# A two-part kernel with a new threshold, shorter routing steps, deferred packing and more output buffers

## The chip, the cores and the metric

The kernel runs on one core of one Trainium2 chip. The metric is the device time of one execution in microseconds; before the change it is 294.05 us (median of three runs, 293.16 to 296.08). TensorE is granted one of two clocks, 1.2 or 2.4 GHz; the profile writes them as 0.50 and 1.00.

## What is computed

A decayed linear attention (4 batches, 8 heads, 768 positions, head size 64) gives 3072 rows of 512 values. A gate gives each row eight logits. All 3072 x 8 logits are walked in falling order, and a row goes to an expert as long as the row is free and the expert has fewer than 384 rows. Each expert is a two-layer network.

```python
    logits = x @ w_gate
    order = np.argsort(-logits.flatten())
    for idx in order:
        tok, e = (int(idx) // E, int(idx) % E)
        if assigned[tok] >= 0 or counts[e] >= cap:   # cap = N // E = 384
            continue
        assigned[tok] = e
        counts[e] += 1
    for e in range(E):
        mask = assigned == e
        h = np.maximum(x[mask] @ w1[e], 0.0)
        out[mask] = h @ w2[e]
```

## The kernel before

**Attention (`_Attn`).** 24 blocks g of 128 rows, six to a batch. Each block is a chain of some thirty operations on all engines: loads on SyncE's queue, splits into high and low halves on ScalarE, VectorE and GpSimd (`sp` lines 1235, 1241 and 1246, `ql` 1218, `xl` 1297, `stl` 1332, `kf` 1161, `vs` 1175, `vl` 1186), matmuls on TensorE, the result `xs` (1277), its store to `x_dram` (1282), and the gate logits, copied by ScalarE (line 1309). The order on each engine is made ahead by `_Plan`: each operation has an engine, a duration, what it depends on and a priority `OFF[name] + g * PERIOD`, and a list scheduler takes the ready operation that can start first. `Router.plan` puts the routing's steps into the same plan, with priorities from `at(g, t)`.

**Early routing (`_Router`).** Column t holds the rows of block t, one on each partition. `scale` (line 113) finds the range of the logits of 8 columns. `level` (line 155) counts how many best logits of 12 columns lie above each of 128 levels (comparison on line 170, twelve matmuls on line 174) and picks the threshold `tau` that 85% pass; lines 187 to 193 make the scale of the digits. A row whose best logit passes goes to its best expert at once; the others are "the rest" and are routed later. `sure` makes the one-hot G of expert or rest, and running counts; `slots` turns them into a place by matmuls (238 to 244) and makes A (line 260), BJ (264), the row numbers R1 (269) and the rows R of the rest (272 to 278); `digits` writes each logit as two half-precision numbers (289 to 302 on VectorE, 289 to 306 on GpSimd for the last two columns). This is done for columns 0 to 15, then 16 to 21. `pack` multiplies A with R1 (line 316) and with R (319) on TensorE; `rows` gives the row numbers of the first 256 rows of each expert, with which GpSimd gathers the rows of jobs 0 and 1 (line 709). Columns 22 and 23 come through `late`, one by one.

**Experts (`_Moe`, `_route_and_moe`).** Jobs 0 to 7 are 256 rows of each expert, jobs 8 to 15 the other 128. A job transposes its rows (727), copies them (`xeT`, 731), multiplies with w1 (745) into PSUM tiles S0 and S1, copies with ReLU (`hT`, 750), multiplies with w2 (761), copies to `oe` (766, ScalarE) and scatters to the output (767, GpSimd). Each `oe` tile is one of four buffers. Gathers, scatters and the loads of the weights (696, 16 of 1 MB) are all issued by GpSimd in order. Meanwhile `steps` routes the rest in seven rounds on VectorE, whose small matmuls are put between the experts' at planned distances (`WAIT`); it gives `perm2`, with which job 8 can gather. `finish` gets the packed sums, and the flag that it leads to sends the kernel into the slow `_exact_path` when a count was out of its bounds.

## Time and profile before

| | us |
|---|---|
| median of three runs | 294.05 |
| lowest, highest | 293.16, 296.08 |
| the profiled execution, device time | 292.14 |
| the profiled execution, span of its instructions | 290.3 |
| mean granted clock in it | 0.92 |

Busy time in the profiled execution: TensorE 231.2 us (80% of the span), VectorE 175.1 (60%), ScalarE 155.2 (53%), GpSimd 180.6 (62%). 52.03 MB are moved. A busy share is a mean over stages with different limits; the rows below are therefore cut into stages. A row of a timeline gives start, duration, engine, line, operation, output<-inputs, shapes and count, and in brackets how long the engine stood idle before and what ended that. One of a wait list gives who waited for whom, the sum, the times and the longest.

### The profile page before, as it was taken

The numbers are of one execution on the slowest core, as the hardware profiler recorded it, in microseconds if no ns is written. First come the engines' busy times: TensorE is split into PE (matmuls) and PEld (weight loads), VectorE is DVE, ScalarE is ACT, GpSimd is POOL, SyncE is SP. The second block draws the span as 40 slices with busy tenths as digits, with TensorE's granted clock in tenths as the row PEclk, the third lists the DMA queues.
The fourth block names the chain that finished last, engine by engine and source line by source line (L and its number), as shares of the span: only waits on it lengthen the run. The fifth ranks groups of instructions, "written<-read, shape, count | busy, mean of one in ns | idle before, by whom it ended". The sixth has DMA issues, their size and how long they took to land.

```text
span 290.3 us, 8655 instructions
## 1 busy us (share of the span) xinstructions
PE 231.2 (80%) x3458; PEld 182.5 (63%) x3471; DVE 175.1 (60%) x572; ACT 155.2 (53%) x297; POOL 180.6 (62%) x225
## 2 busy tenths in 40 slices
PE   1689897999997995985874887886577899899980
PEld 0568786888886875875873645654345566577740
DVE  2569786688989869899955477785566470000000
ACT  5388786788887754673210335325242354466650
POOL 9789798889979965876437783425352145454220
PEclk9999998899999996999555699999998899999996
DMA  6999999999999938999983999999999426333111
GB/s 132 217 218 212 212 234 241 250 232 242 223 262 243 252 91 178 150 216 185 223 177 43 152 190 208 225 228 229 225 232 227 150 86 133 92 92 78 71 76 42
DMA packets 96975, 52.03 MB, mean 179 GB/s; under 512 B 76960, under 2 KB 88224, under 8 KB 96928
## 3 DMA queue, kind: packets, MB, share of 16 engines
q0 software_dynamic: 17920, 26.22, 47.2%
q1 hardware_dynamic: 79008, 25.19, 39.2%
q8 instruction: 29, 0.48, 0.7%
q14 instruction: 18, 0.15, 0.2%
HBM read 58.74 MB, written 12.58 MB: 246 GB/s over the span
## 4 chain that ended last, share of the span: by engine, by line
PE 38%; DMA 20%; DVE 14%; issue 11%; POOL 8%; ACT 5%; SPq 1%; POOLq 0%; ACTq 0%; DVEq 0%
DMA out_dram<-oe,perm 12%; DMA w<-in_moe_w_dram 6%; PE p L761 5%; PE p L745 5%; PE S L1228 5%; PE XL L1268 4%; PE n L1191 3%; PE pt L1191 3%; PE stp L1319 3%; PE pos L1191 3%; POOL xe L709 3%; DVE sp L1241 3%; PE XL L1257 2%; DVE xs L1277 2%; DMA kf<-in_k_dram 2%
## 5 line engine op out<-in xcount | busy, mean ns | idle before, releaser
L745 PE MATMUL p<-xeT,w 128*128 128x256 bf16 (+1 forms) x512 | 51.7, 254 | 8.6 <-ACT hT L750 5.7
L745 PEld LDWEIGHTS <-w 128*128 128x128 bf16 x512 | 40.2, 100 | 17.5 <-issue 10.8
L761 PE MATMUL p<-w,hT 128*128 128x512 bf16 x179 | 45.4, 379 | 7.0 <-ACT oe L766 6.3
L767 POOL DMA_INDIRECT out_dram<-oe,perm x24 | 24.2, 1007 | 41.8 <-ACT oe L766 33.9
L750 ACT ACTIVATE hT<-p 128x512 bf16<-128x512 f32 (+1 forms) x64 | 31.0, 491 | 20.4 <-PE p L745 18.7
L1235 ACT CAST sp<-S 128x512 bf16<-128x512 f32 x48 | 33.7, 747 | 15.2 <-PE S L1228 8.6
L1246 POOL TENSOR_SCALAR_AFFINE_SELECT sp<-sp 128x512 f32<-128x512 f32 x48 | 30.7, 646 | 12.3 <-DVE sp L1241 9.4
L766 ACT COPY oe<-p 128x512 f32<-128x512 f32 x24 | 14.0, 585 | 45.2 <-PE p L761 22.1
L709 POOL DMA_INDIRECT xe<-x_dram,perm x24 | 24.7, 1029 | 21.3 <-PE p L745 4.8
L1241 DVE TENSOR_TENSOR sp<-S,sp 128x512 bf16<-128x512 f32 x48 | 33.7, 741 | 4.2 <-ACT sp L1235 3.5
L761 PEld LDWEIGHTS <-hT 128*128 128x128 bf16 x192 | 16.7, 97 | 23.0 <-issue 8.3
L1161 POOL TENSOR_TENSOR kf<-kf 128x512 f16<-128x512 f32 x24 | 25.9, 1079 | 8.2 <-DMA kf<-in_k_dram 8.2
L1186 POOL TENSOR_TENSOR vl<-vs,vh 128x512 bf16<-128x512 f32 x24 | 27.9, 1161 | 4.0 <-ACT vh L1181 3.7
L1175 POOL TENSOR_TENSOR vs<-vf,lamneg 128x512 f32<-128x512 f32 x24 | 25.1, 1045 | 0.0
L1228 PE MATMUL S<-qh,kT 64*128 64x128 f16 x384 | 22.7, 232 | 1.9 <-DVE sp L1241 1.3
L1268 PE MATMUL XL<-vh,sp 128*128 128x64 bf16 x384 | 23.9, 198 | 0.3 <-POOL sp L1246 0.3
L1277 DVE TENSOR_TENSOR xs<-XL,lampow 128x512 f32<-128x512 f32 x24 | 16.5, 687 | 11.0 <-PE XL L1268 10.9
L1191 PE MATMUL pt<-identf,qf 128*128 128x128 f32 x96 | 16.7, 301 | 8.0 <-DMA qf<-in_q_dram 8.0
L1268 PEld LDWEIGHTS <-sp 128*128 128x128 bf16 x576 | 21.5, 101 | 2.3 <-POOL sp L1246 0.8
L1228 PEld LDWEIGHTS <-kT 64*128 64x128 bf16 (+1 forms) x576 | 18.4, 102 | 5.5 <-issue 3.8
L1268 PE MATMUL XL<-vl,sp 128*128 128x64 bf16 x192 | 21.6, 198 | 0.0
L1191 PE MATMUL n<-identf,xs 128*128 128x128 f32 x96 | 16.7, 300 | 4.2 <-DVE xs L1277 2.1
(269 smaller groups left out, 536.7 us busy)
## 6 DMA issues: line engine op xcount, KB each, us to landing
w<-in_moe_w_dram POOLq DMA_DIRECT2D x16, 1024.0 KB, 14.2
qf<-in_q_dram SPq DMA_DIRECT2D x24, 256.0 KB, 5.1
kf<-in_k_dram SPq DMA_DIRECT2D x24, 256.0 KB, 5.0
vf<-in_v_dram SPq DMA_DIRECT2D x24, 256.0 KB, 5.0
x_dram<-xs SPq DMA_DIRECT2D x24, 256.0 KB, 4.6
xe<-x_dram,perm POOLq DMA_INDIRECT x24, 5.8
out_dram<-oe,perm POOLq DMA_INDIRECT x24, 3.2
lam_sb<-in_lam_dram SPq DMA_DIRECT2D x1, 4.0 KB, 3.1
```

Source lines behind the costliest of these rows:

```text
L709: nc.gpsimd.indirect_dma_start(out=xe[:, c, :], out_offset=None, in_=self.x_dram[0:rows, :], in_offset=bass.IndirectOffsetOnAxis(ap=pm, ax ...
L745: nc.tensor.matmul(p1[:, f, 0:n, :], self.w1t[e][:, kc, fc * P : (fc + 1) * P], j["xeT"][:, kc, 0:n, :], start=(kc == 0), stop=(kc == 3), ...
L750: nc.scalar.activation(hT[:, fp, :, 0:n, :], p1[:, :, 0:n, :], ACT.Relu)
L761: nc.tensor.matmul(p2, j["hT"][:, kc // 2, kc % 2, c, :], self.w2t[e][:, kc, :], start=(kc == 0), stop=(kc == 7), skip_group_check=True)
L1161: self.nc.gpsimd.tensor_tensor(lo, kf.rearrange("p (c j) -> p c j", c=4), self.ksplit(kf)[0], OP.subtract)
L1186: self.nc.gpsimd.tensor_tensor(d["vl"], d["vs"], d["vh"], OP.subtract)
L1191: self.nc.tensor.transpose(ps[:, hp, :], src(hp), self.identf)
L1228: self.nc.tensor.matmul(S[a][:, hp, :], kk[r, hp, :], qq[r, hp, :], start=(i == 0), stop=(i == 2))
L1235: self.nc.scalar.copy(s[:, :, :, 1], d["S"][a])
L1241: self.nc.vector.tensor_tensor(s[:, :, :, 0], d["S"][a], s[:, :, :, 1], OP.subtract)
L1246: self.nc.gpsimd.affine_select(out=sf, in_=sf, compare_op=OP.is_ge, fill=0.0, base=0, pattern=[[0, 4], [1, 128]], channel_multiplier=-1)
L1268: self.nc.tensor.matmul(d["XL"][:, a, hp, :], d["sp"][a][:, hp, :, ss], vv[:, 2 * hp + a, :], start=(first and hp == 0 and i == 0), stop=( ...
```

## The change

- `level` takes the mean over the partitions of the least best logit in columns 0 to 4 as threshold, by one matmul with a matrix of 1/128. `scale` loses its own search and takes its range from the same matmul; it runs as one step after it.
- `sure` compares the logits with max(best, threshold) and has no more index arithmetic. `digits` has four steps in place of seven and runs on VectorE alone, for columns 0 to 21 after the attention (`at(24, 0)`); the rows of the rest (`rest_rows`) are moved there too. Slots are made for columns 0 to 17 and 18 to 21 (before 0 to 15 and 16 to 21).
- `pack` does only the product with R1; the product with R (`gain`) goes into `finish`, and both accumulators share the bank `cnt`.
- `late` is gone: columns 22 and 23 are one piece with the same functions, in `finish`.
- `warm(n)` puts n matmuls of 512 columns, whose result nobody reads, on TensorE: 4, 8 and 6 of them in `finish`, ahead of the transposes of job 0.
- `oe` has seven buffers instead of four.
- PERIOD is 4.4 instead of 4.6, and all offsets are new. Some constants are gone.

```diff
-    NR, NB, CA, CB = 8, 12, 16, 22
+    NR, CA, CB = 5, 18, 22
+    MID, SPAN, TOP = 1536.0, 2.25, 2047.0
...
+    def level(self, L):
...
+        V.reduce_max(self.v[:, 0:n], L[:, 0:n, :], axis=AX.X)
+        yield
+        m2 = rc.tile([P, 2], F32, name="m2")
+        V.tensor_reduce(m2[:, 0:1], self.v[:, 0:n], axis=AX.X, op=OP.min)
+        V.tensor_reduce(m2[:, 1:2], L[:, 0:n, :].rearrange("p t e -> p (t e)"), axis=AX.X,
                         op=OP.min)
         yield
...
+        tp = self.ps.tile([P, 2], F32, tag="cnt", name="tps")
+        nc.tensor.matmul(tp, self.mean, m2, start=True, stop=True)
+        yield
+        self.tb = rc.tile([P, 2], F32, name="tb")
+        V.tensor_copy(self.tb, tp)
+        self.tau = self.tb[:, 0:1]
+
+    def scale(self):
...
+        V.tensor_scalar(zr, self.tb[:, 1:2], self.tau, -self.SPAN, OP.subtract, OP.mult)
+        V.tensor_scalar(zr, zr, 1e-30, None, OP.max)
         self.zlo = rc.tile([P, 1], F32, name="zlo")
...
+        V.tensor_tensor(self.zlo, zr, self.tau, OP.subtract)
         self.zsc = rc.tile([P, 1], F32, name="zsc")
         V.reciprocal(self.zsc, zr)
...
+        V.tensor_scalar(self.zsc, self.zsc, self.TOP, None, OP.mult)
...
+        V.tensor_scalar(u, v, self.tau, None, OP.max)
         yield
         G = rc.tile([P, 9, n], BF16, name=f"G{k}")
...
+        V.tensor_tensor(G[:, 0:8, :], L[:, a:b, :].rearrange("p t e -> p e t"),
+                        u[:, None, :].to_broadcast([P, 8, n]), OP.is_ge)
+        yield
+        V.tensor_scalar(G[:, 8, :], v, self.tau, None, OP.is_lt)
         yield
...
+    def digits(self, L, a, b):
...
+        V.tensor_scalar(Z, L[:, a:b, :].rearrange("p t e -> p e t"), self.zlo, self.zsc, OP.add,
+                        OP.mult)
+        yield
+        V.tensor_scalar(Z, Z, 1.0 / 1024.0, self.TOP, OP.max, OP.min)
+        yield
+        zh = self.zp[:, :, 0, a:b]
+        V.tensor_copy(zh, Z)
+        yield
+        V.tensor_tensor(self.zp[:, :, 1, a:b], Z, zh, OP.subtract)
+        yield
...
     def pack(self, a, b):
 
         nc = self.nc
         if a == 0:
-            self.pe1 = self.ps.tile([128, 16], F32, tag="S0", name="pe1")
-            self.acc = self.ps.tile([128, 76], F32, tag="cnt", name="acc")
+            ct = self.ps.tile([128, 96], F32, tag="cnt", name="pk")
+            self.pe1, self.acc = ct[:, 0:16], ct[:, 16:92]
         for t in range(a, b):
             nc.tensor.matmul(self.pe1, self.A[:, :, t], self.R1[:, :, t], start=(t == 0),
                              stop=(t == self.CB - 1))
+
+    def gain(self, a, b):
+
         for t in range(a, b):
-            nc.tensor.matmul(self.acc, self.A[:, :, t], self.R[:, :, t], start=(t == 0), stop=False,
-                             skip_group_check=True)
+            self.nc.tensor.matmul(self.acc, self.A[:, :, t], self.R[:, :, t], start=(t == 0),
+                                  stop=(t == 23), skip_group_check=True)
...
+        plan.op("sc", 0, "DVE", 0.8, self.scale, [("rs", 3)], self.at(A, 5))
+        chain("d1", self.digits(L, 0, B), (0.35, 0.35, 0.3, 0.35), [("lg", B - 1), ("sc", 0)],
+              self.at(24, 0))
+        chain("x1", self.rest_rows(0, B), (0.5, 1.0), [("s2", 6), ("d1", 3)], self.at(24, 1))
...
+    def warm(self, n):
+        if n:
+            sink = self.ps.tile([128, 512], F32, tag="S1", name="sink")
+        for _ in range(n):
+            self.nc.tensor.matmul(sink, self.identb, self.i_kt.rearrange("p k t -> p (k t)")[:, 0:512],
+                                  start=True, stop=True)
+
     def finish(self, L):
...
+        self.gain(0, B)
+        list(self.sure(L, B, 24, 3))
+        self.warm(4)
+        yield 0.1
+        list(self.slots(B, 24, 3))
+        list(self.digits(L, B, 24))
+        list(self.rest_rows(B, 24))
+        self.warm(8)
+        yield 0.1
+        self.gain(B, 24)
...
+        self.warm(6)
         yield from self.steps(rest)
...
-        oe = self.mp.tile([P, 512], F32, tag="oe", name="oe", bufs=4)
+        oe = self.mp.tile([P, 512], F32, tag="oe", name="oe", bufs=7)
...
-            yield ("land", 0.5)
+            yield ("land", 1.0)
...
-    PERIOD = 4.6
...
+    PERIOD = 4.4
```

## Rows read from the trace of the kernel before

**Rows 1.** The page, chain of work that ended last: shares of the span by engine.

```profile
PE 38%; DMA 20%; DVE 14%; issue 11%; POOL 8%; ACT 5%; SPq 1%; POOLq 0%; ACTq 0%; DVEq 0%
```

**Rows 2.** Stretches: length, busy time (instructions) of each engine, clock, DMA share, GB/s.

```profile
63.83:87.16 23.33, 22.28 (x508) 19.90 (x509) 21.23 (x44) 20.00 (x41) 21.32 (x26) 1.00 1.02 243
87.16:102.70 15.54, 14.04 (x325) 12.45 (x325) 14.64 (x23) 11.93 (x25) 15.35 (x18) 1.00 1.05 248
102.70:112.78 10.08, 6.53 (x111) 4.77 (x109) 7.88 (x13) 3.60 (x8) 6.44 (x8) 0.89 0.55 106
112.78:151.88 39.10, 32.06 (x592) 28.78 (x590) 34.24 (x83) 18.68 (x38) 22.95 (x32) 0.76 1.02 192
151.88:161.38 9.50, 4.07 (x29) 3.20 (x29) 4.23 (x33) 1.18 (x2) 7.00 (x13) 0.50 0.42 53
161.38:231.67 70.29, 55.40 (x463) 37.02 (x469) 45.26 (x264) 25.86 (x41) 31.62 (x33) 0.95 1.10 211
231.67:249.92 18.25, 15.82 (x122) 10.63 (x122) 5.65 (x41) 9.20 (x15) 8.33 (x10) 1.00 0.41 101
249.92:290.30 40.38, 30.85 (x343) 22.32 (x347) 0.00 (x0) 19.71 (x47) 12.80 (x13) 0.93 0.26 74
```

**Rows 3.** Timelines of VectorE and of GpSimd in block 16.

```profile
105.23 0.29 DVE L178 TENSOR_SCALAR_CACHE_REDUCE lscr<-lcnt 128x128 bf16<-128x128 f32 x1 [2.09 <-PE lcnt L174]
107.66 3.97 DVE L189 SCALAR_TENSOR_TENSOR zlo<-zr,mb 128x1 f32<-128x1 f32 x1
...
110.97 0.63 POOL L1246 TENSOR_SCALAR_AFFINE_SELECT sp<-sp 128x512 f32<-128x512 f32 x1
```

**Rows 4.** Timelines of ScalarE, TensorE and GpSimd before the hand-over.

```profile
140.73 0.18 ACT L1309 COPY logits<-n 128x8 f32<-128x8 f32 x1
...
144.68 2.41 PE L319 MATMUL acc<-r_R,r_A 128*128 128x76 f16 x16
147.96 0.67 PE L238 MATMUL pos<-gbase,ones 1*128 1x54 f32 x2
...
154.59 1.16 POOL L709 DMA_INDIRECT xe<-x_dram,perm  x1 [0.80 <-DVE ja L359]
```

**Rows 5.** Waits from 161.38 to 231.67 us (jobs 0 to 5).

```profile
ACT oe L766 <- DMA out_dram<-oe,perm: 20.1, 6, 5.0
...
PE p L745 <- ACT hT L750: 5.7, 3, 2.1
PE p L761 <- ACT oe L766: 4.9, 5, 1.8
```

**Rows 6.** DMA issues from 156 to 228 us: queue, operation, count, median us to landing.

```profile
out_dram<-oe,perm POOLq DMA_INDIRECT x10, 16.5
```

**Rows 7.** Timeline of TensorE, matmuls of jobs 5 and 7.

```profile
223.00 3.36 PE L745 MATMUL p<-xeT,w 128*128 128x256 bf16 x16 [2.09 <-ACT hT L750]
...
240.69 3.69 PE L745 MATMUL p<-xeT,w 128*128 128x256 bf16 x32
...
246.83 1.89 PE L761 MATMUL p<-w,hT 128*128 128x512 bf16 x8 [0.72 <-ACT oe L766]
```

**Rows 8.** Groups by line, VectorE, 112.78 to 151.88 us: busy, mean ns.

```profile
L204 DVE TENSOR_TENSOR r_ohb<-logits,r_v 128x128 bf16<-128x128 f32 (+1 forms) x2 | 1.5, 726 | 0.0
...
L278 DVE TENSOR_TENSOR r_R<-BJ,r_zp 128x1024 f16<-128x1024 f16 (+1 forms) x2 | 1.0, 514 | 0.0
L298 DVE TENSOR_SCALAR H<-H 128x128 f32<-128x128 f32 (+1 forms) x2 | 0.9, 473 | 0.0
...
L207 DVE TENSOR_TENSOR ae<-r_ohb,i_et 128x128 bf16<-128x128 bf16 (+1 forms) x2 | 0.5, 229 | 0.0
L302 DVE CAST r_zp<-H 128x128 f16<-128x128 f32 (+1 forms) x2 | 0.4, 210 | 0.0
```

**Rows 9.** Groups by line and form, TensorE, 153 to 167 us (job 0).

```profile
L745 PE MATMUL p<-xeT,w 128*128 128x256 bf16 x32 | 5.6, 349 | 1.2 <-ACT xeT L731 1.2
```

**Rows 10.** Timeline of GpSimd: last load of weights, first gather of job 8.

```profile
211.65 0.96 POOL L696 DMA_DIRECT2D w<-in_moe_w_dram  x1
...
236.76 1.05 POOL L709 DMA_INDIRECT xe<-x_dram,perm  x1 [3.03 <-DVE t L644]
```

More of the change, by code (lines that the diff above doesn't have):

```diff
@@ L83, in dve_constants @@
             ones[sc] = o
+        self.mean = rc.tile([P, P], F32, name="mean")
+        V.memset(self.mean, 1.0 / 128.0)
         ones3 = rc.tile([3, P], F32, name="ones3")
@@ L234, in slots @@
         V, n = nc.vector, b - a
-        G, cum = (self.G1, self.cum1) if k == 1 else (self.G2, self.cum2)
+        G, cum = self.G[k], self.cum[k]
         pos = self.ps.tile([P, 9, n], F32, tag="pos", name=f"pos{k}")
@@ L238, in slots @@
         nc.tensor.matmul(pos, self.ones3[0:1, :], self.gbase[:, :, a:b], start=True, stop=False)
-        if k == 2:
-            nc.tensor.matmul(pos, self.ones[1],
-                             self.cum1[:, :, self.CA - 1 : self.CA].to_broadcast([P, 9, n]),
+        if k > 1:
+            nc.tensor.matmul(pos, self.ones[1], self.before[:, :, None].to_broadcast([P, 9, n]),
                              start=False, stop=False)
@@ L413, in plan @@
-        V = self.nc and self.nc.vector
-        chain("d1", self.digits(V, L, 0, self.CA, 1), (0.25, 0.2, 0.2, 0.2, 0.2, 0.35),
-              [("c1", 6)], self.at(22, 4))
-        chain("s1", self.slots(0, self.CA, 1),
-              ("P0.35", 0.3, 0.35, 0.4, 1.4, 0.4, 0.3, 0.3, 0.8), [("c1", 6), ("kT", 23)],
-              self.at(23, 1))
-        chain("c2", self.sure(L, self.CA, self.CB, 2), (0.17, 0.2, 0.2, 0.2, 0.17, 0.2, 0.3),
-              [("lg", self.CB - 1), ("c1", 6)], self.at(23, 3))
@@ L421, in plan @@
-        chain("d2", self.digits(V, L, self.CA, self.CB, 2), (0.2, 0.17, 0.17, 0.17, 0.17, 0.3),
-              [("lg", self.CB - 1), ("d1", 5)], self.at(23, 9))
-        chain("s2", self.slots(self.CA, self.CB, 2),
-              ("P0.4", 0.2, 0.2, 0.4, 0.6, 0.25, 0.2, 0.25, 0.45), [("c2", 6), ("s1", 2)],
-              self.at(23, 4))
-        plan.op("pk", 0, "PE", 1.7, lambda: self.pack(0, self.CA),
-                [("s1", 8), ("d1", 5), ("spl0", 23), ("sph0", 23), ("stl", 22), ("sth", 22)],
-                self.at(23, 9))
@@ L429, in plan @@
-        plan.op("pk", 1, "PE", 0.7, lambda: self.pack(self.CA, self.CB),
-                [("pk", 0), ("s2", 8), ("d2", 5)], self.at(23, 5))
+        A, B = self.CA, self.CB
+        chain("rs", self.level(L), (0.2, 0.4, "P0.2", 0.17), [("lg", self.NR - 1), ("dc", 2)],
+              self.at(10, 0))
+        chain("c1", self.sure(L, 0, A, 1), (0.25, 0.2, 0.4, 0.2, 0.9),
+              [("lg", A - 1), ("rs", 3), ("dc", 6)], self.at(A + 4, 0))
+        chain("s1", self.slots(0, A, 1), ("P0.5", 0.3, 0.4, 0.6, 1.9, 0.5, 0.5),
+              [("c1", 4), ("kT", 23)], self.at(A + 4, 2))
@@ new lines, in plan @@
+        chain("c2", self.sure(L, A, B, 2), (0.17, 0.17, 0.2, 0.17, 0.35), [("lg", B - 1), ("c1", 4)],
+              self.at(B, 0))
+        chain("s2", self.slots(A, B, 2), ("P0.4", 0.2, 0.2, 0.5, 0.5, 0.25, 0.25),
+              [("c2", 4), ("s1", 1)], self.at(B, 1))
+        plan.op("pk", 0, "PE", 1.3, lambda: self.pack(0, A),
+                [("s1", 6), ("stl", 22), ("sth", 22)], self.at(B + 1, 3))
+        plan.op("pk", 1, "PE", 0.4, lambda: self.pack(A, B), [("pk", 0), ("s2", 6)], self.at(B, 5))
```

276 lines of the change are left out of this document (47 added, 229 removed).

## The prediction

> **What bounds the kernel now.** I read the page first. Its chain of waits gives TensorE 38%, DMA 20% and VectorE 14% of the span [rows 1], so no single engine is the limit, and the share of busy time says little: the run has to be cut into stages. The cuts are the starts of ScalarE's copies of the gate logits (one per block of 128 rows) and of the first matmul of some expert jobs; the table of stretches has one row for each [rows 2].
>
> From the logits of block 7 to those of block 12 five blocks take 23.33 us, 4.67 us each, with TensorE busy 22.28 us: this is the pace of the attention loop when nothing disturbs it. Blocks 13 to 15 take 15.54 us (5.18 each). Block 16 alone takes 10.08 us, and the last seven take 39.10 us (5.59 each) with VectorE busy 34.24 us of it. Against 4.67 us a block that is 1.5, 5.4 and 6.4 us lost, 13.3 us in all.
>
> Why block 16 is late stands in the timelines of VectorE and GpSimd [rows 3]. VectorE first waits 2.09 us for the twelve counting matmuls of `level`, and then one instruction on 128x1 elements, zlo at line 189, lasts 3.97 us. It ends at 111.63 us; GpSimd, which had worked without a gap since 106.25 us, ends its last mask at 111.60 us. So the long instruction is a wait for GpSimd to fall idle, and everything behind it on VectorE (xl, then the gate) stands.
>
> Then the hand-over, from the last logits (151.88 us) to the first matmul of expert job 0 (161.38 us): 9.50 us at a granted clock of 0.50, with DMA at 0.42 [rows 2]. Its order [rows 4]: the logits of block 21 are there at 140.73 us, TensorE packs accumulators for 16 columns from 144.68 us for 2.41 us, only then comes the slot matmul of columns 16 to 21 (147.96), and the first gather goes out at 154.59.
>
> Last the experts. Jobs 0 to 5 (256 rows each) take 70.29 us, 11.7 each, with TensorE busy 55.40 us; jobs 6 and 7 take 18.25 us, 9.1 each; the eight small jobs and the end take 40.38 us [rows 2]. What stands between 11.7 and 9.1 is in the list of waits [rows 5]: ScalarE's copy into `oe` waits 20.1 us in six waits for a scatter to land, because there are four `oe` buffers and a scatter takes 16.5 us to land in this stretch [rows 6], nearly the time of two jobs. ScalarE works in order, so the ReLU copies behind it are late, and TensorE waits 5.7 us for `hT` and 4.9 us for `oe`. After the last of these waits 16 matmuls of 256 columns take 3.36 us, while 32 of them take 3.69 us in job 7 [rows 7].
>
> **The change, part by part.** *Threshold* (`level`, `scale`). The counting matmuls, the 1536-element comparison and some twenty small VectorE steps go; four VectorE steps and one matmul of two columns replace them, on blocks 0 to 4, when GpSimd and VectorE have the same load as in the undisturbed stretch. I take block 16 to run at 4.67 us plus 0.5 us for what is left: -4.9 us. Bounds: nothing gained if the wait only moves, -5.4 if it goes wholly. Blocks 13 to 15 carried `ylev`, `qlev` and the comparison; of their 1.5 us lost I credit 1.0.
>
> *Fewer VectorE steps before the hand-over* (`sure`, `digits`, `rest_rows`). In the seven last blocks the seven digit groups of lines 289 to 302 cost 4.5 us, the outer product of line 278 1.0 us, and ten small steps of 0.23 us or less (lines 207, 210, 216, 272, 274, two each) 2.1 us [rows 8]: 7.6 us leave the stretch. Two `is_lt` steps and the five of `scale` come in, seven of about 0.2 us, 1.4 us. The new G reads the same strided logits as line 204 (0.73 us mean [rows 8]) and takes its place. VectorE then needs 34.24 - 6.2 = 28.0 us for seven blocks, 4.0 each, and is no longer the limit. I take 5.1 us a block, since the offsets of all operations are new: 39.1 - 35.7 = -3.4 us. Bounds: 0, and -6.4 at the undisturbed pace.
>
> So the last logits come 9.3 us earlier, at 142.6 us.
>
> *Order of the hand-over* (`pack`, `gain`, `finish`). `pack` keeps the 16-column product alone, digits leave GpSimd, so the slot matmul need not wait 2.41 us and the gathers can start some 6 us after the logits of block 21, before the last logits. This does not move job 0 by itself: the new `finish` puts on TensorE, ahead of the transposes of job 0, the 22 products of `gain` (16 took 2.41 us at the low clock [rows 4], so 3.3), the slots of the last two columns with VectorE on both sides of them, and 18 fillers of 512 columns. The filler's price is in [rows 7]: 256 columns pass in 3.69 / 32 = 0.115 us at the high clock and in 3.36 / 16 = 0.21 us at the low one, so 512 columns in 0.23 or 0.42 us: 4.1 to 7.6 us for 18, of which those that run while VectorE works are free. Chain after the last logits: six small steps of `sure` 1.2 us, slot matmuls 0.6, seven steps of `slots` 1.5, digits and rows of two columns 1.3, last products and six fillers 1.7 to 2.9, transposes and copy 2; with `gain` and the first fillers partly in front, 9 to 13 us, against 9.50 now. I take 11: +1.5 us. Bounds -2 and +5.
>
> The fillers' return: job 0 ran its 32 up-matmuls in 5.6 us [rows 9], behind a hand-over at 0.50, against 3.69 us in job 7. I take -1.7 us. The Trainium skill, "TensorE: Matmul & The Clock Gate", Part 1, says that the array is at half rate by default and that activity releases it; by that rule the fillers would give all of 1.9 us here, and the trace agrees as far as that the clock stood at 0.50 through the idle hand-over.
>
> *Seven `oe` buffers.* A buffer comes round after 3.5 jobs, some 35 us, against 16.5 us to land: the six waits go. TensorE gets back the 5.7 us of `hT`, of the 4.9 us for `oe` (five waits) what exceeds the 0.7 us that a second chunk waits in job 7 too [rows 7], 1.4, and the half-speed matmuls there, 3.36 - 1.7: -8.8 us. Bounds -5 and -11. Nothing else takes over at once: the routing's result sends the first gather of job 8 out at 236.76 us [rows 10], 13 us before that job's first matmul, and the routing, whose matmuls stand between those of the experts, moves with them.
>
> Sum: -4.9 - 1.0 - 3.4 + 1.5 - 1.7 - 8.8 = -18.3 us, span 272.0. Outside the span lie 292.14 - 290.3 = 1.84 us, so 273.8, say **274 us**. The median of the runs is 1.9 us above the profiled execution; a median may come out that much higher too.
>
> **Rivals.** *Weights bind the experts.* DMA is busy without a break while jobs 0 to 5 run (1.10 of its engines [rows 2]). If loads and not buffers set the pace, the 7.1 us of waits come back as waits for weights. Against: the last load is issued at 211.65 us [rows 10], over 29 us before job 7's second half uses it, and gathers and loads would start some 14 us earlier. Time 281; chance 0.13.
>
> *The attention gains nothing*, the new offsets giving back what VectorE saves: 274 + 9.3 = 283; chance 0.12.
>
> *The wait for GpSimd comes back.* `scale` still has five 128x1 steps, `sure` one, and each can be caught as line 189 was: +4 us, 278. The Trainium skill, "SBUF — State Buffer", Who interferes with whom, has VectorE and GpSimd share a port pair that whoever comes first holds for its whole instruction; the ends of line 189 and of GpSimd's mask, 0.03 us apart, fit it, and it speaks against putting digits on VectorE. Chance 0.08.
>
> *The hand-over shrinks as well*: fillers all hidden, last columns done before the gathers land, attention at 4.67 us a block: -3 more, -3.5 more, 266; chance 0.12.
>
> *Slower.* All thirty offsets and the period are new. Without the attention's part the change still brings 9.0 us; so if the new order makes the attention loop slower than now by more than that, the kernel is slower. That is 0.4 us a block over 24 blocks, and 0.5 us (12 us in all) for 1%: from block 7 to the end the mean pace is 88.05 / 16 = 5.5 us now, so it decides from a mean pace of 6.0 us, and the time is 295 or more. Block 16 shows that one bad wait costs 5 us, but it would have to come in more than two blocks and the old one not go. Chance 0.06. That the threshold sends the kernel into its exact path (some 8 x 161 rounds of fifteen VectorE steps of 0.15 us or more, an estimate of 3 ms) I can nearly exclude: from the inputs, 426 tokens stay below the new threshold where 512 are allowed, the fullest expert has 361 of 384, the emptiest 273 early where 256 are needed.
>
> *No effect*: buffers and threshold both give back what they win, 292; chance 0.03.
>
> **The numbers.** My forecast has 0.46, with its own range 270 to 279. The others as said. All but the last two are faster by over 1% (about what a measurement here can tell from no change): 0.91; within 1%: 0.03; slower: 0.06. From 264 to 285 us the cases hold a little over 0.8; beyond it lie the two last ones, a hand-over that gains still more, and an attention that loses a little.
>
> **What would show it.** Right: block 16 at about 5 us and no VectorE step of several us in it; VectorE below nine tenths in the last seven blocks; the last logits at 142 to 144 us; first gather before them; no ScalarE wait for a scatter; jobs 1 to 5 at about 10 us each; the same 40 us at the end. Wrong: waits of TensorE for weights, the last logits later than 148 us, or job 0 starting more than 13 us after them.

## The result, and the profile after

The changed kernel takes 273.6 us (median of four runs, 272.3 to 276.44), the kernel before beside it 293.61 us: a ratio of 0.9345, with a 95% interval of 0.920 to 0.949. Medians are over all executions; ratios, here and below, are over each kernel's faster ones alone, those within 1.5% of its fastest. The forecast was 274 us. The profiled execution took 272.3 us with a span of 270.4 us, against 292.14 and 290.3 us before.

The stretches after, cut at the same events as [rows 2], with the start of the program to block 7 ahead of them (columns: from and to, length, busy time of TensorE, its weight loads, VectorE, ScalarE and GpSimd with instructions, clock, DMA share, GB/s):

```profile
0.00:61.81 61.81, 47.81 (x977) 41.48 (x977) 40.57 (x83) 44.45 (x84) 52.02 (x72) 1.00 1.00 206
61.81:85.46 23.65, 22.48 (x510) 20.43 (x510) 19.50 (x36) 20.04 (x40) 22.87 (x28) 1.00 1.02 237
85.46:100.33 14.87, 14.33 (x350) 13.06 (x348) 11.95 (x20) 13.05 (x27) 14.22 (x17) 1.00 1.07 248
100.33:103.97 3.64, 3.16 (x75) 2.78 (x70) 3.21 (x6) 2.96 (x8) 2.49 (x4) 1.00 0.97 259
103.97:135.25 31.28, 26.46 (x574) 23.50 (x573) 27.70 (x56) 18.37 (x39) 24.85 (x30) 0.94 1.11 223
135.25:149.91 14.66, 10.58 (x61) 6.96 (x62) 8.25 (x48) 1.18 (x2) 9.55 (x10) 0.66 1.18 216
149.91:212.29 62.38, 52.43 (x468) 35.70 (x474) 45.86 (x272) 26.69 (x42) 26.82 (x28) 1.00 1.16 226
212.29:230.53 18.24, 15.29 (x118) 10.25 (x117) 2.90 (x18) 8.61 (x15) 8.32 (x9) 1.00 0.42 102
230.53:270.40 39.87, 30.84 (x343) 22.32 (x347) 0.00 (x0) 20.10 (x47) 12.86 (x13) 0.93 0.27 75
```

Beside [rows 2], with what the prediction had for each (in us):

| stretch | before | after | difference | predicted |
|---|---|---|---|---|
| start to the logits of block 7 | 63.83 | 61.81 | -2.0 | 0 |
| blocks 8 to 12 | 23.33 | 23.65 | +0.3 | 0 |
| blocks 13 to 15 | 15.54 | 14.87 | -0.7 | -1.0 |
| block 16 | 10.08 | 3.64 | -6.4 | -4.9 |
| blocks 17 to 23 | 39.10 | 31.28 | -7.8 | -3.4 |
| last logits to job 0 (hand-over) | 9.50 | 14.66 | +5.2 | +1.5 |
| jobs 0 to 5 | 70.29 | 62.38 | -7.9 | -10.5 (buffers 8.8, clock of job 0 1.7) |
| jobs 6 and 7 | 18.25 | 18.24 | 0.0 | 0 |
| eight small jobs and the end | 40.38 | 39.87 | -0.5 | 0 |
| sum | 290.30 | 270.40 | -19.9 | -18.3 |

So the total came out, and its parts did not. Up to the last logits the change brought 16.6 us, not 9.3; from there to job 6 it brought 2.7 us, not 9.0. An error of 7.3 us and one of 6.3 us the other way hide each other: that the forecast was met so closely is luck.

The chain of waits shows where the time stands now. DMA had 20% of it [rows 1], nearly all of that scatters and weights of the expert jobs; here DMA has 7%, most of it loads of k in the attention, and GpSimd has 18%. The 6% of SyncE's queue lie in the first 16 us, where it issues the first loads of q, k and v one after the other:

```profile
PE 38%; POOL 18%; DVE 13%; issue 11%; DMA 7%; SPq 6%; ACT 5%; POOLq 0%; ACTq 0%; DVEq 0%
```

In this execution VectorE has no step of several microseconds left. Its longest small steps in blocks 16 to 23 are these three (timeline: start, length, line; compare zlo in [rows 3]):

```profile
110.79 1.24 DVE L148 TENSOR_SCALAR r_u<-r_v,tb 128x18 f32<-128x18 f32 x1
...
115.00 1.48 DVE L151 TENSOR_TENSOR G<-logits,r_u 128x144 bf16<-128x144 f32 x1
...
125.96 1.30 DVE L191 TENSOR_SCALAR ja<-slot 128x18 f32<-128x18 f32 x1
```

The new hand-over, from the chain of waits of the changed kernel (start, length, engine, what):

```profile
135.25 0.17 ACT logits L1182
...
137.07 0.80 DVE r_R L237
137.87 0.10 DVE perm L260
138.01 3.24 PE pk L255 x22
...
141.47 1.48 PE sink L318 x3
142.96 0.54 PE pos L176 x2
...
146.99 1.31 PE sink L318 x6
...
148.84 1.02 ACT xeT L604
```

It is one chain of steps, none beside another: logits (135.25), VectorE's row products for 22 columns up to 137.87, the step `perm` behind them, then on TensorE the 22 products of `gain` (3.24 us at half clock) and three fillers, and only behind these the slot matmul of the last two columns (142.96), for which VectorE had stood idle 5.06 us. VectorE's timeline of the changed kernel, the row numbers of columns 18 to 21 and the end of that wait:

```profile
136.61 0.18 DVE L206 TENSOR_TENSOR r_R<-r_BJ,idh 128x64 f16<-128x64 f16 x1
...
143.73 0.18 DVE L185 TENSOR_TENSOR sl<-pos,G 128x18 f32<-128x18 f32 x1 [5.06 <-PE pos L181]
```

The first two gathers, one for each half of job 0's rows, leave at 138.23 and 139.62 us, three and four microseconds after the last logits, as GpSimd's timeline of the changed kernel shows:

```profile
138.23 1.08 POOL L582 DMA_INDIRECT xe<-x_dram,perm  x1 [9.35 <-DVE G L154]
139.62 1.03 POOL L582 DMA_INDIRECT xe<-x_dram,perm  x1 [0.30 <-issue]
```

### The profile page after: what moved, and what is told of

Read it like the earlier page. It is cut to its first block, busy times and chain, and to the rows that moved or that the text cites. A ratio compares the mean times of both kernels' runs of the same rounds, so it can differ in the third digit from the quotient of the medians.

```text
span 270.4 us, 8606 instructions
## 1 busy us (share of the span) xinstructions
PE 223.4 (83%) x3458; PEld 176.5 (65%) x3472; DVE 159.9 (59%) x533; ACT 155.4 (57%) x297; POOL 174.0 (64%) x204
## 4 chain that ended last, share of the span: by engine, by line
PE 38%; POOL 18%; DVE 13%; issue 11%; DMA 7%; SPq 6%; ACT 5%; POOLq 0%; ACTq 0%; DVEq 0%
PE p L634 11%; PE p L618 9%; DMA kf<-in_k_dram 6%; SPq L1028 5%; POOL vl L1059 4%; POOL sp L1119 4%; POOL kf L1034 4%; POOL vs L1048 3%; PE n L1064 2%; ACT oe L639 2%; PE stp L1192 2%; PE XL L1141 2%; DVE ind L423 2%; POOL out_dram L640 2%; PE XL L1130 2%
## 5 line engine op out<-in xcount | busy, mean ns | idle before, releaser
L618 PE MATMUL p<-xeT,w 128*128 128x256 bf16 (+1 forms) x512 | 48.6, 245 | 3.3 <-ACT xeT L604 2.1
L618 PEld LDWEIGHTS <-w 128*128 128x128 bf16 x512 | 38.6, 97 | 11.0 <-issue 5.8
L623 ACT ACTIVATE hT<-p 128x512 bf16<-128x512 f32 (+1 forms) x64 | 31.2, 491 | 21.6 <-PE p L618 16.6
L1114 DVE TENSOR_TENSOR sp<-S,sp 128x512 bf16<-128x512 f32 x48 | 33.1, 738 | 4.2 <-ACT sp L1108 3.0
L1034 POOL TENSOR_TENSOR kf<-kf 128x512 f16<-128x512 f32 x24 | 25.1, 1048 | 11.3 <-DMA kf<-in_k_dram 11.2
L1150 DVE TENSOR_TENSOR xs<-XL,lampow 128x512 f32<-128x512 f32 x24 | 16.5, 689 | 13.3 <-PE XL L1141 12.6
L1141 PE MATMUL XL<-vh,sp 128*128 128x64 bf16 x384 | 22.8, 195 | 0.0
L604 ACT COPY xeT<-pt 128x1024 bf16<-128x1024 bf16 (+1 forms) x16 | 12.8, 798 | 17.0 <-PE pt L600 14.9
L1101 PE MATMUL S<-qh,kT 64*128 64x128 f16 x384 | 20.9, 221 | 0.3 <-ACT kT L1075 0.3
L1141 PE MATMUL XL<-vl,sp 128*128 128x64 bf16 x192 | 20.8, 195 | 0.0
L1064 PE MATMUL pos<-identf,kf 128*128 128x128 f32 x96 | 15.7, 288 | 4.7 <-POOL kf L1034 4.7
```

The source lines that it names most:

```text
L618: nc.tensor.matmul(p1[:, f, 0:n, :], self.w1t[e][:, kc, fc * P : (fc + 1) * P], j["xeT"][:, kc, 0:n, :], start=(kc == 0), stop=(kc == 3), ...
L623: nc.scalar.activation(hT[:, fp, :, 0:n, :], p1[:, :, 0:n, :], ACT.Relu)
L1034: self.nc.gpsimd.tensor_tensor(lo, kf.rearrange("p (c j) -> p c j", c=4), self.ksplit(kf)[0], OP.subtract)
L1064: self.nc.tensor.transpose(ps[:, hp, :], src(hp), self.identf)
L1114: self.nc.vector.tensor_tensor(s[:, :, :, 0], d["S"][a], s[:, :, :, 1], OP.subtract)
L1141: self.nc.tensor.matmul(d["XL"][:, a, hp, :], d["sp"][a][:, hp, :, ss], vv[:, 2 * hp + a, :], start=(first and hp == 0 and i == 0), stop=( ...
```

## The experiments

Theory after the result: the last blocks gained more because VectorE's load and the new order of the operations work together; the hand-over is long because of the order on TensorE; the large jobs gained by the buffers. Rivals: the offsets alone made the attention; gathers and not TensorE's order end the hand-over; something other than the buffers shortened the jobs. Where these runs are read by stretches, it is the stretch of the profiled execution; the attention loop varies more than the edits, as the last section tells.

**Four buffers in the changed kernel.**

```diff
-        oe = self.mp.tile([P, 512], F32, tag="oe", name="oe", bufs=7)
+        oe = self.mp.tile([P, 512], F32, tag="oe", name="oe", bufs=4)
```

> The changed kernel with four oe buffers instead of seven, all else as it is. My theory: the buffers are worth what the large jobs lost to them, 8.8 us less the part of it that was a slow clock. ScalarE's copies into oe wait for scatters again, jobs 0 to 5 take about 70 us instead of 62.4, and the time is 280 to 282 us. Rival: the loads and not the buffers set the pace of the large jobs now that they start 11 us earlier; then four buffers cost under 2 us and the time stays at 274 to 275.

Measured: 275.02 us, ratio to before 0.944 (0.921 to 0.966). Jobs 0 to 5 take 64.36 us, 2.0 more than with seven buffers; ScalarE waits 8.5 us for scatters in three waits, where it waited 20.1 us in six before [rows 5] and waits 2.0 us in one with seven buffers. The row of that stretch in the run with four buffers:

```profile
148.88:213.24 64.36, 53.40 (x474) 35.91 (x474) 46.14 (x272) 26.46 (x42) 26.86 (x28) 1.00 1.13 220
```

And a line of its list of ScalarE's waits (total, times, longest):

```profile
ACT oe L639 <- DMA out_dram<-oe,perm: 8.5, 3, 4.0
```

The theory falls: in the changed kernel the buffers are worth 2.0 us, not 8.8. The price is the rival's; its reason, that the loads set the pace, is not shown by it.

**Six buffers in the kernel before** (the same edit from 4 to 6).

> The kernel before with six oe buffers instead of four (seven leave too little memory for it), nothing else. My theory: six buffers come round after three jobs, 30 us, against 16.5 us for a scatter to land, so the six waits of ScalarE go and the stretch of jobs 0 to 5 falls from 70.3 to 62 or 63 us: 0.970 to 0.978 of the time before, 286 us. Rival: the large jobs of the kernel before, which start at 161 us, are bound by something else as well (hand-over, loads), so that half or less comes back: 290 us.

Measured: 285.71 us (281.88 to 288.17) against 291.78 us (286.44 to 292.60) of the kernel before beside it, in this run and in the two with the kernel before below. The ranges overlap, so these three are read by their stretches. Jobs 0 to 5 fall from 70.29 to 62.71 us, and no wait for a scatter is left in ScalarE's list, though a scatter still takes 16.1 us to land. The row of that stretch in the run with six buffers:

```profile
162.01:224.72 62.71, 54.34 (x463) 36.34 (x469) 45.54 (x264) 26.47 (x41) 31.59 (x33) 0.97 1.17 217
```

And the scatters in its list of DMA issues, same stretch (median us to landing last):

```profile
out_dram<-oe,perm POOLq DMA_INDIRECT x11, 16.1
```

So in the kernel that the prediction looked at six buffers are worth 7.6 us in that stretch, near the 8.8 us worked out for seven. The two runs together say that the six waits have more than one remedy, and that the change brings another one beside the buffers.

**The kernel before with half the weights.**

```diff
     def load_w(self, m):
+        if m >= 8:
+            return
     # in room(): experts 4 to 7 take the tiles of experts 0 to 3
```

> The kernel before, with four oe buffers as it has, but without the weight loads of experts 4 to 7: these take the weights of experts 0 to 3, so half of the 16 MB is not loaded and their rows are computed with the wrong weights. My theory: a scatter takes 16.5 us to land only because it stands behind megabytes of weights in the same engines; without those loads the six waits of ScalarE for a scatter go although there are four buffers, jobs 0 to 5 take 62 to 63 us instead of 70.3, and the time is 284 to 286 us. Rival: 128 rows of 2 KB written one by one take that long by themselves; the waits stay and the time is 291 us or more.

Measured: 287.71 us, ratio 0.990 (0.986 to 0.994); in the profiled execution the last logits came 1.5 us later than in that of the kernel before, and the eight small jobs and the end took 43.03 us instead of 40.38, for a reason that stays open; so the total stays above the expected 284 to 286. The stretch is as the theory says: jobs 0 to 5 take 62.02 us with four buffers, there is no wait for a scatter, and a scatter lands in 2.8 us, not 16.5 [rows 6]. The row of the stretch in the run with half the weights:

```profile
162.80:224.82 62.02, 54.17 (x469) 36.37 (x469) 44.77 (x264) 26.48 (x41) 24.89 (x25) 0.97 0.50 104
```

And the scatters in its list of DMA issues, same stretch:

```profile
out_dram<-oe,perm POOLq DMA_INDIRECT x11, 2.8
```

Scatters are slow because they stand behind weights. All three, loads, gathers and scatters, are on one queue (q0 on the page of each of these profiles). The Trainium skill, "DMA: Bandwidth & Descriptors", Two DMAs through the same engine are not ordered, says that within one queue of one DMA engine descriptors start in order; the 2.8 against 16.5 us agree with it.

What the change does to this besides the buffers: when job 0 starts, 7.40 MB have gone through that queue in the run with four buffers, 6.77 MB in the kernel before; the longer hand-over has let more weights through. That this is why three of the six waits went is argued from those two numbers and not shown by a run.

**No fillers** (the three calls of `warm` out).

> The changed kernel without its 18 filler matmuls. My theory: of the fillers three of 1.48 us and six of 1.3 us stand on the chain between the last logits and job 0, so the first matmul of job 0 comes 2.5 to 3 us earlier, while the clock stays at 0.50 longer and job 0's 32 up-matmuls take 5.6 us instead of 3.8, and its transposes 0.5 us more: 273 to 274 us, no difference that can be told. Rival: the fillers earn more than they cost, since the low clock would last through the whole of job 0 and its down-matmuls (7 us at half speed): 276 to 277.

Measured: 273.87 us, ratio 0.941 (0.924 to 0.958), as the theory has it in the total. The hand-over is 13.36 us instead of 14.66 (the theory had 2.5 to 3 us less), job 0 takes 12.26 us instead of 10.77: 1.3 us saved, 1.5 us lost (the granted clock in job 0 is 0.85, with fillers 1.00). The run shows something else, too. With the fillers gone TensorE still does not start on job 0's transposes when the last products are done (145.0 us): it waits until 145.82 us. The first four transposes take the first gather, whose issue ended at 138.93 us, 6.9 us before; in the kernel before they took it up 2.4 us after its issue (from 155.75 to 158.17 us). GpSimd's timeline without fillers, the first gather:

```profile
137.84 1.09 POOL L579 DMA_INDIRECT xe<-x_dram,perm  x1 [9.80 <-DVE G L154]
```

TensorE's timeline without fillers, the last products, the transposes and the start of job 0:

```profile
144.52 0.44 PE L255 MATMUL pk<-r_R,r_A 128*128 128x76 f16 x2 [2.94 <-DVE r_R L237]
...
145.82 1.24 PE L597 MATMUL pt<-identb,xe 128*128 128x128 bf16 x8 [0.83 <-DMA xe<-x_dram,perm]
148.22 3.57 PE L615 MATMUL p<-xeT,w 128*128 128x256 bf16 x16 [1.16 <-ACT xeT L601]
```

**Slots ahead of gain, twelve fillers fewer.**

```diff
     def finish(self, L):
-        self.gain(0, B)
         list(self.sure(L, B, 24, 3))
-        self.warm(4)
+        late = self.slots(B, 24, 3)
+        next(late)
+        self.gain(0, B)
         yield 0.1
-        list(self.slots(B, 24, 3))
+        list(late)
         list(self.digits(L, B, 24))
         list(self.rest_rows(B, 24))
-        self.warm(8)
```

> The changed kernel with the slot matmuls of the last two columns put on TensorE ahead of the 22 products of gain, and without the first twelve fillers (six stay, behind the last products). My theory: the hand-over of 14.66 us is long because VectorE waits 5.06 us for those slot matmuls, which stand in TensorE's order behind the gain products and three fillers. With the order turned VectorE's steps run beside the gain products, job 0's first matmul comes 4 to 5 us earlier, some 10 us after the last logits, and the time is 269 to 270 us. Rival: job 0's gathers, which leave only after the last logits into DMA engines that are full with weights, land no earlier than 145 us; then TensorE waits for them and at most 1.5 us are gained, 272 to 273.

Measured: 271.07 us, ratio 0.928 (0.911 to 0.945). The hand-over is 12.43 us, between theory and rival, and job 0 takes 12.72 us at a clock of 0.80. The wait of VectorE for the slot matmul is gone, but TensorE now stands before the transposes until 148.02 us, 6.0 us after the first gather's issue had ended (142.07 us). TensorE's order was a cause of the long hand-over, and right behind it stood the gather.

**Two weight loads behind the first gathers**, on top of that order and without fillers.

```diff
-        for m in range(6):
+        for m in range(4):
-        plan.op("lw", 6, "Pool", 0.9, lambda: moe.load_w(6), [("ga", 1)], 0)
+        plan.op("lw", 4, "Pool", 0.9, lambda: moe.load_w(4), [("ga", 1)], 0)
```

> The changed kernel with the slot matmuls of the last two columns ahead of gain, without fillers, and with two weight loads (both of expert 2) put behind the first gathers instead of ahead of them. My theory by now: with the order on TensorE turned, the hand-over ends on the landing of job 0's second gather, and that is late because it stands in the DMA engines behind weights: in the run with the slots first TensorE took it up 4.6 us after its issue had ended, without fillers 5.5 us, in the kernel before, whose engines were at 0.42, 2.5 us. With two loads fewer in front it takes 2.5 to 3 us, the hand-over falls from 12.4 to 10 or 10.5 us, and the time is 269 to 270 us. Rival: a gather of 128 rows takes 4.6 us or more on a chain of its own; then the hand-over stays at 12.4 us and the time at 271 us or above.

Measured: 271.08 us, ratio 0.934 (0.928 to 0.940). The expectation had taken the second gather's issue and the first one's landing together; counted for one gather, the first, the issue ends at 143.58 us and TensorE takes it up at 146.81, after 3.2 us instead of 6.0 or 6.9. The hand-over is 9.83 us, with DMA at 0.41 in it, where it was 1.18 in the changed kernel. GpSimd's timeline with the late loads, the first gather:

```profile
142.48 1.10 POOL L581 DMA_INDIRECT xe<-x_dram,perm  x1 [11.45 <-DVE G L154]
```

TensorE's timeline with the late loads, the transposes and the start of job 0:

```profile
146.81 1.36 PE L599 MATMUL pt<-identb,xe 128*128 128x128 bf16 x8 [0.42 <-DMA xe<-x_dram,perm]
149.32 3.57 PE L617 MATMUL p<-xeT,w 128*128 128x256 bf16 x16 [1.16 <-ACT xeT L603]
```

The theory holds for the stretch: from the last logits to job 6 it takes 73.4 us, against 77.0 in the changed kernel. The total does not show it, for in this profiled execution the last logits came at 139.49 us, 4.2 us later than in that of the changed kernel, whose loop is the same but for two loads. That the loads had more time to drain because of this is not the cause: in the next run the last logits come later still (141.57 us), with six loads ahead, and the first gather is taken up about 7 us after its issue (from 145.63 to 152.58 us). Blocks 17 and 18 are 4.9 us longer here than in the changed kernel; in block 18 one small step of VectorE lasts 3.47 us, as its timeline with the late loads shows:

```profile
112.37 3.47 DVE L148 TENSOR_SCALAR r_u<-r_v,tb 128x18 f32<-128x18 f32 x1
```

**Fillers in the gaps.** The order with the slots first, with four fillers each behind the gates of blocks 21 and 23 and ahead of the transposes.

```diff
+        for i, g in enumerate((21, 23)):
+            plan.op("fw", i, "PE", 0.9, lambda: self.warm(4), [("gate", g)], 0)
```

> The changed kernel with the slot matmuls of the last two columns ahead of gain and twelve fillers in three other places: four behind the gate of block 21, where TensorE stands idle 1.80 us, four behind the gate of block 23, where it stands idle 1.63 us, four ahead of job 0's transposes. My theory: the clock falls to 0.50 in just these idle stretches; with work in them it stays at 1.00, the 22 products of gain take 1.9 us instead of 3.2 to 3.6, job 0 takes 10.8 us instead of 12.7, and the time is 268.5 to 270 us, 2 us below the run with the slots first. Rival: the idle stretches are not where it falls (it falls from execution to execution at other places), the hand-over stays at 0.50 and the fillers there cost what they take: 271 to 273 us.

Measured: 273.05 us, ratio 0.931 (0.927 to 0.934). In the profiled execution blocks 11 and 12 took 6.4 us more than in the changed kernel, in code that is the same. One step of `scale` on 128x1 elements lasts 5.20 us there, until GpSimd's operation ends (83.14 us), as VectorE's timeline shows:

```profile
77.95 5.20 DVE L135 TENSOR_TENSOR zlo<-zr,tb 128x1 f32<-128x1 f32 x1
```

Behind the last logits the hand-over is 13.42 us at a clock of 0.50, and job 0 takes 12.11. The theory finds no support.

**Both of them.**

> The two edits before this one together: slots first, twelve fillers in the gaps, two weight loads behind the first gathers. If both theories hold the hand-over is about 9.5 us with job 0 at 10.8 us, and the time 267 to 268.5 us. If only the loads count, 269 to 270; if neither does, 271 or more.

Measured: 269.82 us, ratio 0.931 (0.926 to 0.936). The hand-over is 10.62 us, and 73.7 us go from the last logits to job 6: the loads count, the fillers in the gaps do not. The clock fell at about 136 us in spite of the fillers behind block 21's gate; TensorE's stretches of 2 us (busy, clock, DMA share, GB/s) in the run with both:

```profile
134.00:136.00 2.00, 2.00 (x35) 0.96 0.22 81
136.00:138.00 2.00, 2.00 (x15) 0.50 0.00 0
```

The four fillers behind block 23's gate take 1.87 us, half clock. The timeline of TensorE shows the products of `gain` still at 3.55 us, and in job 0 a wait of 1.60 us for VectorE:

```profile
139.51 3.55 PE L255 MATMUL pk<-r_R,r_A 128*128 128x76 f16 x24
...
152.22 0.54 PE L436 MATMUL cps<-oh,ind 128*128 128x8 bf16 x4 [1.60 <-DVE ind L425]
```

**The checks spread.** VectorE was late there because of eleven small steps for the final flag in the first round of the routing. They go into later rounds, in four pieces.

```diff
-                if i == 1 and r == 0:
-                    rest()
+                if i > 1 and r == 1:
+                    next(rest, None)
```

> The run before (slots first, twelve fillers in the gaps, two late weight loads) with one more edit: the eleven small VectorE steps of rest() in finish, which prepare the final flag and stand in one piece in the first round of the routing, are spread over later rounds in four pieces. My theory: with the shorter hand-over job 0 still takes 12.25 us instead of 10.8, because TensorE's next counting matmuls stand 1.60 us waiting for VectorE, which works through these eleven steps first (149.7 to 151.8 us in that run). Spread out they cost nothing there: job 0 takes 10.8 us, and the time falls by 1 to 1.5 us to 268.5. Rival: the routing is behind anyway, so the wait moves to the next counting matmuls or to the wait of the later pieces, and the time stays at 269.5 to 270.

Measured: 271.49 us, ratio 0.939 (0.930 to 0.948). Job 0 falls from 12.25 to 10.94 us, as expected, and jobs 1 to 4 rise from 40.2 to 42.6 us. TensorE's waits for VectorE in these jobs go from 2.6 to 3.8 us, half of that rise: the rival, as far as this shows; the other half is open.

**The old offsets in the changed kernel** (PERIOD and OFF of the kernel before).

> The changed kernel with the period and the thirty offsets of the kernel before. My theory: most of the 16.6 us that the attention gained comes from the threshold and from the VectorE steps that went, not from the order; with the old offsets the last logits come at 137 to 140 us instead of 135.3, and the time is 275 to 278 us. Rival: the new offsets made most of the gain beyond the 9.3 us that I had worked out; then the last logits come at 142 us or later and the time is 281 or more.

Measured: 281.64 us, ratio 0.966 (0.951 to 0.982). The last logits come at 146.36 us, 11.1 us later: the rival. Block 16 takes 4.69 us, so the new offsets are not what frees it. No small VectorE step is held for longer than 1.64 us; the time goes in blocks 17 and 21 and behind (rows of those stretches), after a wait of TensorE of 2.58 us, and at a falling clock. The stretches of block 17, of block 21, and of blocks 22 and 23 in the run with the old offsets:

```profile
105.20:115.64 10.44, 7.31 (x112) 6.73 (x113) 5.20 (x9) 6.41 (x13) 9.09 (x12) 0.84 1.05 177
...
127.64:138.20 10.56, 6.48 (x118) 5.74 (x117) 7.95 (x14) 3.18 (x7) 6.73 (x7) 0.73 1.15 227
138.20:146.36 8.16, 5.92 (x88) 4.98 (x89) 6.19 (x25) 1.50 (x5) 0.00 (x0) 0.50 0.90 184
```

That wait in its timeline of TensorE:

```profile
108.43 0.22 PE L1192 MATMUL stp<-vl,kf 128*128 128x128 bf16 x1 [2.58 <-POOL vl L1059]
```

**The new offsets in the kernel before.**

> The kernel before with the period and the thirty offsets of the changed kernel, nothing else. My theory: the offsets alone are worth little where block 16 still waits for the threshold: the last logits come at 147 to 152 us (151.88 before), the time is 290 to 294 us. Rival: the new offsets carry the attention by themselves: last logits at 143 us or earlier, 285 us or less.

Measured: 287.92 us against 291.78 us beside it. The last logits come at 148.74 us, 3.1 us earlier, as the theory has it, while the total stays below its 290 to 294. In the last seven blocks VectorE is busy 34.07 us of 37.00, as it was in the kernel before (34.24 of 39.10 [rows 2]): it stays the busiest engine there. But one scan of 144 elements (line 221) lasts 4.49 us of that, where the two of that line together took 1.4 us before; a held step is in this busy time. The row of the last seven blocks with the new offsets in the kernel before:

```profile
111.74:148.74 37.00, 28.55 (x573) 25.52 (x572) 34.07 (x72) 17.09 (x36) 22.82 (x33) 0.85 1.10 208
```

That step in VectorE's timeline there:

```profile
127.94 4.49 DVE L221 TENSOR_TENSOR_SCAN cum<-m,G 128x144 bf16<-128x144 f32 x1
```

**The kernel before with a given threshold.**

```diff
-        y = rc.tile([P, n], F32, name="ylev")      # and all of level's counting
+        self.tau = tau = rc.tile([P, 1], F32, name="tau")
+        V.memset(self.tau, 0.0357331)
```

> The kernel before with the threshold given as a constant (0.0357331, the value that it works out itself): the comparison of 1536 elements, the twelve counting matmuls and six small VectorE steps are left out, the two steps for zlo and those for zsc stay. My theory: block 16 falls from 10.1 us to about 5 and the last blocks gain too because the clock does not fall behind it; the last logits come 5 to 8 us earlier, 286 to 289 us. Rival: the wait of VectorE for GpSimd only moves to the next small step (zlo still among them): a step of several us stays, and the time is 292 us or more.

Measured: 290.26 us against 291.78 us beside it. The last logits come at 150.02 us, 1.9 us earlier. The rival's mechanism holds, while the total lies between the two: zlo is no longer held, but the comparison of line 184 (line 204 before, 0.73 us mean in [rows 8]) now lasts 5.24 us. It ends at 109.66 us; GpSimd, which had worked without a gap, ends its last operation at 109.50 us. Blocks 16 and 17 take 8.01 and 10.20 us. VectorE's timeline with the given threshold:

```profile
104.42 5.24 DVE L184 TENSOR_TENSOR r_ohb<-logits,r_v 128x128 bf16<-128x128 f32 x1
```

GpSimd's timeline there, the first and the last operation that this step met:

```profile
104.17 1.06 POOL L1140 TENSOR_TENSOR kf<-kf 128x512 f16<-128x512 f32 x1
...
108.47 1.03 POOL L1154 TENSOR_TENSOR vs<-vf,lamneg 128x512 f32<-128x512 f32 x1
```

And the stretches of blocks 16 and 17:

```profile
102.80:110.81 8.01, 3.23 (x83) 2.67 (x82) 8.01 (x8) 3.48 (x9) 7.61 (x9) 0.86 1.02 206
110.81:121.01 10.20, 9.29 (x117) 8.72 (x115) 7.58 (x17) 5.40 (x10) 4.94 (x7) 0.61 0.89 153
```

## Why the prediction was right in its sum and wrong in its parts

**Threshold (-4.9; measured -6.4 in block 16).** The step that failed is the reason, not the sign: that the wait goes because the threshold's steps go. Taking the steps out alone only hands the wait to the next small VectorE step, which the prediction had as the lower bound of this term and, with 4 us and a chance of 0.08, as a rival for the changed kernel. In the changed kernel VectorE has fewer steps besides, and in its profiled execution none of the small ones in blocks 16 to 23 is held for more than 1.48 us; which part of the change does it is not shown, but it is not the new offsets (4.69 us for block 16 with the old ones). And the rival is not gone: with the late loads and with the fillers in the gaps it came, 3.47 us on line 148 and 5.20 us on line 135, one of the five steps that it named.

**Blocks 17 to 23 (-3.4; measured -7.8, beyond the bound of -6.4).** VectorE's need was worked out as 28.0 us, and it was busy 27.70 us. That this came so close is in part luck: the five steps of `scale`, counted in, ran at 77.7 us in block 11, and three steps were held, by about 1 us each. The mis-sized term is the pace taken after it, 5.1 us a block "since the offsets are new"; it was 4.47, below the undisturbed 4.67. The 2 x 2 of last logits shows what it rests on:

| last logits, us | old offsets | new offsets |
|---|---|---|
| kernel before | 151.88 | 148.74 |
| changed kernel | 146.36 | 135.25 |

The offsets alone bring 3.1 us, the rest alone 5.5, both together 16.6. In the one execution of each mixed kernel, VectorE is busy through nearly all of the last blocks where it has its old steps, and TensorE runs into idle stretches and half clock where the order is the old one. Between programs with one and the same loop the last logits move by 3.8 us (below), so the 3.1 and 5.5 are rough; the excess of 8.0 us over their sum is more than twice that. The medians of whole runs show the same direction and half the size: the new offsets take 8.0 us off the changed kernel (281.64 to 273.6) and 3.9 off the kernel before (291.78 to 287.92). One part of it could have been read ahead: [rows 2] give the seven blocks a clock of 0.76 and TensorE 32.06 us of work; after, it is 0.94 and 26.46 us. The prediction counted the low clock in job 0 and had no term for it here.

**The start (0; measured -2.0).** Not foreseen. Old offsets with the new kernel and new offsets with the old one both reach block 7 at 61.8 to 62.2 us, so either half seems to do it; but programs with the changed kernel's loop reach it at 60.80 to 63.18 us, and which operation it is stays open.

**Hand-over (+1.5, bounds -2 and +5; measured +5.2).** This is the step that the prediction itself had marked: job 0 more than 13 us after the last logits. Two statements failed. First, that gathers start some 6 us after the logits of block 21, ahead of the last logits; they started 11.6 us after the former and 3.0 after the latter. Most of that goes before `perm`: VectorE takes the slot steps of columns 18 to 21 between those of blocks 22 and 23 and, at the end, behind a step that waits for the last logits themselves (135.45), so their row numbers (line 206) are there at 136.79 us, 10.1 us after the logits of block 21. Then `perm` stands behind the row products of all 22 columns (0.80 us). Second, that products and fillers lie beside VectorE's work: the slot matmul of the last columns stands behind them in TensorE's order, so 3.24 and 1.48 us came one after the other with it. And one thing was not in the sum at all: the attention ends earlier but the weight loads do not, so the first gathers now enter engines at a share of 1.18, where they had met 0.42 [rows 2]. In the changed kernel itself this does not show, since the transposes start behind the last fillers without a wait; it is what holds the hand-over next. The first gather is taken up 6.9 us after its issue without fillers, 2.4 us before the change, and 3.2 us with two loads moved.

**Fillers (-1.7 in job 0).** Job 0 took 10.77 us, 1.1 less than before (11.88) and 1.5 less than without them; their cost on the way, which the prediction had in its sum of the hand-over, was 1.3 us. In sum nothing.

**Seven buffers (-8.8; measured 2.0).** Right for the kernel before, where six buffers bring 7.6 us. Wrong for the changed kernel, where the same six waits are already halved by the other parts. The term was priced on the trace of before as if the other edits left its cause, a queue full of weights, as it was.

**The rest of the list.** Right: jobs 1 to 5 at 10.0 to 10.7 us, the same 40 us at the end, no wait of TensorE for weights, VectorE below nine tenths in the last seven blocks (27.70 of 31.28 us). Wrong: the last logits at 142 to 144 us (135.25), the first gather before them, no ScalarE wait for a scatter (one of 2.0 us is left), and the sign of being wrong that did come, job 0 more than 13 us after the last logits. The rival of the shrinking hand-over has a wrong sum: 273.8 - 3 - 3.5 is 267.3, not 266. Of the rivals, "weights bind the experts" did not come as such; but it is weights that held the scatters before and that hold the first gathers after.

**A better version.** The late loads shorten the way from the last logits to job 6 from 77.0 to 73.4 and 73.7 us in two runs, with the slots first; the slots first without them leave it at 76.4. With the checks spread as well it is 75.4. As a whole, 269.82 us with both edits against 273.6 us of the changed kernel, at ratios to before of 0.931 (0.926 to 0.936) and 0.9345 (0.920 to 0.949), is probably a gain of 1%, and the intervals do not prove it.

## What to carry to other kernels

Price an edit against the kernel that the other edits leave, not against the trace alone: a wait with two remedies is paid back once, and a limit with two causes may give way only when both go. Where a stage is pulled forward, ask what else starts with it and what does not: here the loads stayed where they were, and the gathers of the next stage came to stand behind them. And add up a hand-over in program order, engine by engine, before calling any of it covered.

## What the runs showed of the hardware

*A held VectorE step outlasts several GpSimd operations.* 3.97 us on 128x1 elements before [rows 3]; 5.24 us on 128x128 in the kernel before with a given threshold, through six GpSimd operations back to back; 3.47 us on 128x18 with the late loads; 5.20 us on 128x1 with the fillers in the gaps. All four end 0.01 to 0.16 us behind the end of a GpSimd operation. The Trainium skill, "SBUF — State Buffer", Who interferes with whom, says that a two-input step of VectorE contends with GpSimd's reads and that whoever comes first has the ports for its whole instruction. The trace agrees on the pair of engines; by that rule the step would wait for the one GpSimd operation that runs, 1.06 us, and in the run with the given threshold it lasted until the last of the six had ended.

*One loop takes different times in single executions, and the clock goes with it.* Four programs with the same loop (the changed kernel, four buffers, no fillers, slots first) had their last logits at 135.25, 134.23, 134.86 and 137.99 us. In two of them one and the same wait can be followed: TensorE stands for `vl` in block 17, 1.53 us in the changed kernel, where the clock stays at 1.00, and 2.47 us in the run with the slots first, where it falls to 0.50 and the block takes 8.92 us instead of 5.27. Why the wait is longer there stays open. The wait in TensorE's timeline of the changed kernel:

```profile
105.17 0.22 PE L1192 MATMUL stp<-vl,kf 128*128 128x128 bf16 x1 [1.53 <-POOL vl L1059]
```

The same wait with the slots first:

```profile
105.20 0.26 PE L1192 MATMUL stp<-vl,kf 128*128 128x128 bf16 x1 [2.47 <-POOL vl L1059]
```

And the stretches of 2 us around it there, all engines:

```profile
104.00:106.00 2.00, 0.80 (x8) 0.80 (x8) 0.62 (x2) 0.00 (x0) 2.00 (x3) 0.58 1.10 252
106.00:108.00 2.00, 2.00 (x23) 1.67 (x23) 0.69 (x1) 1.11 (x3) 2.00 (x4) 0.50 0.83 166
```

Such a loop has to be compared by stretches, or over many executions; one profile of each version would have called the slots-first order slower (272.9 against 270.4 us of span), and its median is the lower of the two.
